# Rotating query and key tiles in three GpSimd instructions, two of them held until VectorE's last two-operand instruction

## The chip, the cores and the metric

The kernel runs on one core of a Trainium2 chip. The metric is the device time of one execution in microseconds (us). TensorE (PE) multiplies matrices, VectorE (DVE) and GpSimd (POOL) do elementwise work and reductions, ScalarE (ACT) applies functions and copies, SyncE (SP) issues DMAs.

## The reference

Attention with rotary positions over 4 batches of 8 heads, 576 tokens and 64 values a head, followed by a gated feed-forward layer.

```
q_rot, k_rot = rotate(q), rotate(k)      # x1*cos - x2*sin, x1*sin + x2*cos
scores = scale * q_rot @ k_rot^T
attn = exp(scores - max(scores)); attn = attn / (sum(attn) + 1e-9)
x = attn @ v                             # heads side by side: 512 wide
h = relu(x @ w_in)
conv = 3-tap convolution of h along the tokens, weights conv_w
out = (h * sigmoid(conv)) @ w_out
```

The feed-forward weights arrive as 64-bit floats and are turned into 32-bit ones on the chip.

## The kernel before

Two heads make a pair; there are 16 pairs (p = 0 to 15). A pair takes five turns: four for 128 query rows of both heads, one for the last 64 rows of both. Turn 5p + s is step s of pair p. In a turn TensorE computes the scores (`emit_S`, tile `sp`), VectorE takes their maxima (`negm`, L264), ScalarE the exponentials (`st` or `str`, L268), TensorE transposes them (`emit_T`, L316), ScalarE copies them out (`pt`, L196), and TensorE multiplies them by v (`emit_E`, L393).

The order is written by hand. `at(turn, rank, fn)` puts work into a table, and the loop at the end of `emit` runs a turn's entries by rising rank; each engine gets its instructions in that order and takes them in that order. Ranks used here: 0 transposes of the exponentials, 0.2 maxima, 0.3 exponentials, 0.4 conversion of weights, 0.45 transposes of rotated q and k, 0.5 scores of the next turn, 1.7 normalisation (L411), 4.5 reciprocal row sums (L362 to L364), 16 loads, 18 rotations.

Up to turn 25 (`WIDE` is 26) the turns also carry the conversion of the weights: for each piece of 512 columns a ScalarE step (L599) and four VectorE steps (L602, L608, L613, L618). Pieces of the last weight matrix are then split: ScalarE makes `wouth` (L685) and GpSimd the remainder `woutl` in four instructions (L682). The split is deferred by a few steps of the table after the piece's L618.

The rotation of pair p (`rope`, tiles `rq` and `rk`) is done by GpSimd in place. The two half-vectors of a head are multiplied by a table of cosines and sines (L187, six pieces of 192 columns), then one product is added to the other (L190, three pieces of 192 columns). VectorE transposes the result into `qT` (L229) and `kT` (L232, with two small ones at L236), which the scores of the pair read. With n = 5p, for pairs 2 to 5 the rotations of both tensors stand at turn n-6, rank 18, the transpose of q at turn n-4 and that of k at turn n-2. Each of `rq` and `rk` has one buffer: the load for pair p+1 waits for the transpose of pair p.

Of the kernel before, what the change touches and what calls it, by code (L numbers as in the profile page):

```python
# [12 lines left out]
ALU = mybir.AluOpType  # L13
# [7 lines left out]
def attention_moe_kernel(ctx, tc, q, k, v, w_in, conv_w, w_out, tab, tabx, out):  # L21
    nc = tc.nc
# [8 lines left out]
    XW = HS + 2  # L31
# [29 lines left out]
    tabt = keep.tile([128, S // 32, 2, 32], F32, name="tabt")  # L61
# [14 lines left out]
    late = {"tail": False, "u": 0}  # L76
# [5 lines left out]
    def defer(k, fn, rank=1):  # L82
        due.setdefault(slot[0] + k, []).append((rank, len(due.get(slot[0] + k, [])), fn))
# [9 lines left out]
    def after(fn):  # L93
        if "m" in psum or late["n"] + 1 == WIDE:
            fn()
        else:
            at(late["n"] + 1, 0.35, fn)

    def spare(n):
        a = free["at"]  # L100
        if "m" in psum or late["n"] + 1 == WIDE:
            return t_tile()[:, 0:n]
        assert a + n <= 960
        free["at"] = a + n
        return free["ps"][:, a:a + n]
# [8 lines left out]
    def m_tile():  # L114
        if late["tail"]:
            return psum["t"].tile([128, 512], F32, tag="mt", name="mt")
        ps = m_pair()
        pair["k"] ^= 1
        return ps[1 - pair["k"]]

    raw = {}
# [21 lines left out]
    def load(p, part):  # L143
        b, hp = divmod(p, NPB)
        x = raw[p, part] = p1.tile([128, S // 32, 2, 32], F32, tag="r" + part, name="r" + part)
        for h in range(2):
            y = (q if part == "q" else k)[b, 2 * hp + h].rearrange("(c i) d -> i c d", i=32)
            for g in range(2):
                r = slice(64 * h + 32 * g, 64 * h + 32 * g + 32)
                nc.sync.dma_start(out=x[r].rearrange("i c e d -> i c (e d)"), in_=y)  # L150
# [3 lines left out]
    def load_v(p):  # L154
        b, hp = divmod(p, NPB)
        t = vmain[p] = p1.tile([128, 2, 4, D], F32, tag="vm", name="vm", bufs=2)
        for h in range(2):
            nc.sync.dma_start(out=t[:, h], in_=v[b, 2 * hp + h, 0:512, :].rearrange("(t p) d -> p t d", p=128))
            nc.sync.dma_start(out=vrem[p % 2][64 * h:64 * h + 64, h, :], in_=v[b, 2 * hp + h, 512:S, :])
# [23 lines left out]
    def rope(p, part):  # L183
        x = raw[p, part]
        for a in range(0, 18, 3):
            y = x[:, a:a + 3]
            nc.gpsimd.tensor_tensor(out=y, in0=y, in1=tabt[:, a:a + 3], op=ALU.mult)  # L187
        for a in range(0, 18, 6):
            y = x[:, a:a + 6]
            nc.gpsimd.tensor_tensor(out=y[:, :, 0, :], in0=y[:, :, 0, :], in1=y[:, :, 1, :], op=ALU.add)  # L190

    QT, KT = {}, {}

    def evac(eng, out, in_, sc=None):
# [30 lines left out]
    def emit_TQ(p, part):  # L225
        qk_tiles(p)
        x = raw.pop((p, part))[:, :, 0, :]
        if part == "q":
            nc.vector.transpose(out=QT[p].rearrange("p (c i) -> p c i", i=32), in_=x)  # L229
        else:  # L230
            kt = KT[p].rearrange("p (c i) -> p c i", i=32)
            nc.vector.transpose(out=kt[:, 2:20], in_=x)  # L232
            if p * STEPS < WIDE:
                for h in range(2):
                    r = slice(64 * h, 64 * h + 64)
                    nc.vector.transpose(out=krem[p % 2][r, r].rearrange("p (c i) -> p c i", i=32), in_=x[r, 16:18])  # L236
            if p * STEPS + STEPS > WIDE:
                nc.vector.transpose(out=kt[:, 0:2], in_=x[:, 16:18])
# [3 lines left out]
    negm, sums = {}, {}  # L242
# [113 lines left out]
    rb = {}  # L356
    rds = {}

    def emit_rinv(p):
        rv = rvc[p % 2]  # L360
        rt = p1.tile([128, 32], F32, tag="rt", name="rt")
        nc.vector.scalar_tensor_tensor(out=rv[:, 0:9], in0=sums[p], scalar=1e-9, in1=sums[p], op0=ALU.add, op1=ALU.max)  # L362
        nc.vector.reciprocal(out=rv[:, 0:9], in_=rv[:, 0:9])
        nc.vector.transpose(out=rt, in_=rv)  # L364
        d = scr.tile([9, 128], F32, tag="d", name="rd")
        for i in range(0, 128, 32):
            nc.sync.dma_start(out=d[:, i:i + 32], in_=rt[i:i + 9, :])
        rds[p] = d
# [15 lines left out]
    def x_at(sl, e):  # L384
        return xT[:, sl, e, :] if sl < NSLOT - NK else xmore[sl][e]

    def emit_E(p, j, a=0, n=XW):
        b, hp = divmod(p, NPB)
        xp = m_tile()[:, 0:n] if "m" in psum else spare(n)
        o = (S - XW) * j  # L390
        for i in range(5):
            for h in range(2):
                nc.tensor.matmul(  # L393
                    out=xp[64 * h:64 * h + 64, :],
                    lhsT=vmain[p][:, h, i, :] if i < 4 else vrem[p % 2][:, h, :],
                    rhs=pt[:, 2 * i + h if i < 4 else 8, o + a:o + a + n],
                    start=(i == 0),
                    stop=(i == 4),
                )
        if a == 0:  # L400
            xns[p, j] = p2.tile([128, XW], F32, tag="xn", name="xn", bufs=4)
        xn = xns[p, j]
        after(lambda: nc.scalar.activation(out=xn[:, a:a + n], in_=xp, func=AF.Copy))

        def norm():
            if plain(2 * b):
                dst = xraw[hp, j] = xtra.tile([128, XW], F32, tag="x", name="xr")
            else:
                xslot[b, hp, j] = free_slots.pop(0)
                dst = xn  # L410
            nc.vector.tensor_tensor(out=dst, in0=xn, in1=rb[p][:, o:o + XW], op=ALU.mult)  # L411

        def high():
            nc.scalar.activation(out=x_at(xslot[b, hp, j], 0), in_=xn, func=AF.Copy)  # L414

        def low():
            sl = xslot[b, hp, j]
            nc.gpsimd.tensor_tensor(out=x_at(sl, 1), in0=xn, in1=x_at(sl, 0).bitcast(F32), op=ALU.subtract)  # L418

        def both():  # L420
            norm()
            if not plain(2 * b):
                defer(1, lambda: (high(), low()))

        norms[p, j] = both

    def plain(blk):
        return blk < 2
# [163 lines left out]
    def to_f32(pool, bufs, w64, n, t=None):  # L592
        w32 = w64.bitcast(I32).rearrange("p (n t) -> p n t", t=2)
        h, l = w32[:, :, 1], w32[:, :, 0]
        if t is None:
            t = pool.tile([128, n], I32, tag="wt", name="wt", bufs=bufs)[0:w64.shape[0]]

        def first():
            nc.scalar.activation(out=t.bitcast(F32), in_=h.bitcast(F32), func=AF.Abs)  # L599

        def clamp():
            nc.vector.tensor_scalar(  # L602
                out=t.bitcast(F32), in0=t.bitcast(F32), scalar1=bits(F32_TINY), scalar2=bits(F32_HUGE),
                op0=ALU.max, op1=ALU.min,
            )

        def shift():
            nc.vector.tensor_scalar(  # L608
                out=t, in0=t, scalar1=3, scalar2=0x3FFFFFFF, op0=ALU.logical_shift_left, op1=ALU.bitwise_and
            )  # L610

        def low():
            nc.vector.scalar_tensor_tensor(  # L613
                out=t, in0=l, scalar=29, in1=t, op0=ALU.logical_shift_right, op1=ALU.bitwise_or
            )

        def third(w):
            nc.vector.scalar_tensor_tensor(  # L618
                out=w.bitcast(I32), in0=h, scalar=-(1 << 30), in1=t, op0=ALU.bitwise_and, op1=ALU.bitwise_or
            )  # L620

        return first, clamp, shift, low, third

    def bits(i):
        import struct

        return struct.unpack("<f", struct.pack("<I", i))[0]
# [98 lines left out]
    WIDE = 26  # L726
# [16 lines left out]
    def at(n, rank, fn):  # L743
        plan.setdefault(n, []).append((rank, len(plan.get(n, [])), fn))

    def emit():
        with tc.manual_schedule(engines=engines):
# [30 lines left out]
            for p in range(1, NP):  # L778
                n = STEPS * p
                early = n - 10 >= WIDE - 1  # L780
                for i, part in enumerate("qk"):
                    if p > 1:
                        at(max(n - 10, WIDE) if early else n - 9 + 2 * i, 19.6 if early else 16, lambda p=p, part=part: load(p, part))
                    at(n - 8 + i if early else max(n - 6, 0), 18, lambda p=p, part=part: rope(p, part))
                    at(n - 5 + i * (n - 15 < WIDE) if early else max(n - 4 + 2 * i, 2), 0.45, lambda p=p, part=part: emit_TQ(p, part))
                at(n - 1, 15, lambda p=p: load_v(p))
            for p in range(NP):
                n = STEPS * p
# [45 lines left out]
            n = -1  # L834
# [38 lines left out]
            for u in seq + second + m2_units(t, B * S // 128):  # L873
                u()
                tick()

    emit()


# [43 lines left out]
```

## Time and profile before

| | us |
|---|---|
| median of 3 runs (473.62 to 475.83) | 473.81 |
| profiled execution | 472.73 |
| its span | 470.9 |

| engine | busy us | share of the span |
|---|---|---|
| PE, matmul | 456.7 | 97% |
| DVE | 354.6 | 75% |
| ACT | 327.4 | 70% |
| POOL | 291.7 | 62% |

The profile is of one execution. Its span runs from the first to the last instruction; the execution's time is 1.83 us longer. TensorE was granted its full clock throughout. The work of the changed rotations lies in the first fifth of the span. Releasers, written `<-`, name what ended an engine's idle time.

### The profile page before, as it was taken

Reading aid. Unit: us, or ns where it says so; the run is one execution under the profiler, and the core shown is the slowest. Engines: PE = TensorE matmul, PEld = TensorE weight load, DVE = VectorE, ACT = ScalarE, POOL = GpSimd, SP = SyncE. Lnnn points to the kernel's source line nnn. Section 1 sums busy time; section 2 is a strip of 40 time slices with the busy share of each in tenths; the row PEclk is TensorE's granted clock in tenths of the full one; section 3 lists DMA queues with packets and bytes.
Section 4 is the critical chain, followed back from the end, with each engine's and each line's share of the span. In section 5 each row is a group of like instructions: output and inputs, shape, how many; then the busy total and the mean of one; then the engine's idle time right before and its main releaser. Section 6 shows DMA issues by size and latency. Waiting matters only on the chain.

```text
span 470.9 us, 12238 instructions
## 1 busy us (share of the span) xinstructions
PE 456.7 (97%) x4555; PEld 357.4 (76%) x4555; DVE 354.6 (75%) x648; ACT 327.4 (70%) x940; POOL 291.7 (62%) x471
## 2 busy tenths in 40 slices
PE   8799999989999999999999999999999999999997
PEld 7356656657666878778787979788787878899886
DVE  6999999968999897678686777866765748368921
ACT  3889879978897878868696868768686844244400
POOL 0977696996889695997949393929420333133510
PEclk9999999999999999999999999999999999999999
DMA  9989667453370715126161716133010000100011
GB/s 242 242 187 227 159 149 147 121 140 82 98 194 6 139 38 124 32 58 102 39 139 39 139 38 139 39 97 79 27 49 27 25 26 3 46 23 24 0 68 45
DMA packets 103631, 42.33 MB, mean 90 GB/s; under 512 B 94524, under 2 KB 97876, under 8 KB 103572
## 3 DMA queue, kind: packets, MB, share of 16 engines
q1 hardware_dynamic: 103120, 41.20, 37.4%
q8 instruction: 36, 0.59, 0.5%
q10 hardware_dynamic: 452, 0.35, 0.2%
q14 instruction: 23, 0.19, 0.1%
HBM read 36.74 MB, written 4.79 MB: 88 GB/s over the span
## 4 chain that ended last, share of the span: by engine, by line
PE 70%; ACT 11%; DVE 10%; POOL 3%; DMA 3%; issue 1%; SPq 1%; ACTq 0%; DVEq 0%; POOLq 0%
PE sp L256 11%; PE mt L552 11%; PE pm L572 10%; PE pm L393 10%; PE pm L460 9%; PE mt L460 7%; PE tp L316 6%; ACT st L268 4%; PE pm L450 4%; DVE negm L264 3%; ACT pt L196 3%; PE sp L393 2%; POOL rk L187 2%; DVE c L481 1%; DMA rk<-k 1%
## 5 line engine op out<-in xcount | busy, mean ns | idle before, releaser
L264 DVE TENSOR_REDUCE negm<-sp 128x1 f32<-128x576 f32 x144 | 102.5, 747 | 23.7 <-PE sp L256 18.9
L268 ACT ACTIVATE st<-sp,negm 128x576 f32<-128x576 f32 x128 | 93.8, 742 | 27.9 <-DVE negm L264 24.0
L256 PE MATMUL sp<-kT,qT 64*128 64x288 f32 (+4 forms) x556 | 94.8, 450 | 0.5 <-ACT pt L196 0.3
L196 ACT ACTIVATE pt<-tp 128x512 f32<-128x512 f32 (+3 forms) x176 | 84.5, 534 | 5.6 <-PE tp L316 5.0
L481 DVE SCALAR_TENSOR_TENSOR c<-rr,cw,c 128x288 f32<-128x288 f32 x128 | 79.7, 623 | 4.2
L187 POOL TENSOR_TENSOR rq<-rq,tabt 128x192 f32<-128x192 f32 x90 | 61.1, 711 | 27.8 <-DMA rq<-q 25.8
L499 POOL TENSOR_TENSOR gm<-c,gm 128x288 fp32r<-128x288 f32 (+4 forms) x72 | 45.7, 640 | 49.8 <-ACT gm L498 49.5
L256 PEld LDWEIGHTS sp<-kT,qT 64*128 64x128 f32 (+1 forms) x556 | 44.8, 174 | 22.6 <-issue 8.6
L187 POOL TENSOR_TENSOR rk<-rk,tabt 128x192 f32<-128x192 f32 x90 | 58.9, 688 | 2.5 <-DVE negm L264 1.8
L316 PEld LDWEIGHTS tp<-idf,st 64*128 64x128 f32 x1024 | 41.4, 139 | 21.4 <-ACT st L268 10.1
L316 PE MATMUL tp<-idf,st 64*128 64x64 f32 x1024 | 47.7, 227 | 5.7 <-ACT st L268 4.9
L393 PE MATMUL pm<-pt,vm 128*64 128x290 f32 x368 | 49.8, 411 | 0.4 <-ACT pt L196 0.4
L572 PE MATMUL pm<-wouth,gm 64*128 64x256 f32 x512 | 49.6, 284 | 0.0
L490 DVE SCALAR_TENSOR_TENSOR c<-c,rr 128x288 f32<-128x288 f32 x64 | 37.2, 602 | 10.3 <-ACT c L487 10.3
L479 DVE TENSOR_SCALAR c<-rr,cw 128x288 f32<-128x288 f32 x56 | 24.4, 436 | 22.7 <-ACT rr L471 22.4
L572 PEld LDWEIGHTS pm<-wouth,gm 64*128 64x128 f32 x512 | 41.4, 186 | 0.0
L418 POOL TENSOR_TENSOR xT<-xn,xT 128x290 fp32r<-128x290 f32 x18 | 16.4, 911 | 37.4 <-ACT xT L414 37.4
L393 PEld LDWEIGHTS pm<-pt,vm 128*64 128x64 f32 x368 | 25.5, 136 | 17.8 <-ACT pt L196 1.0
L460 PE MATMUL pm<-xT,wh 128*128 128x290 f32 x176 | 37.0, 302 | 0.0
L572 PE MATMUL pm<-woutl,gm 64*128 64x256 f32 x256 | 36.8, 278 | 0.0
L487 ACT ACTIVATE c<-c 128x288 f32<-128x288 f32 x64 | 28.5, 445 | 11.4 <-DVE c L481 11.4
L450 PE MATMUL pm<-xr,wr 128*128 128x290 f32 x128 | 34.5, 417 | 0.0
(137 smaller groups left out, 971.3 us busy)
## 6 DMA issues: line engine op xcount, KB each, us to landing
rq<-q SPq DMA_DIRECT2D x60, 144.0 KB
rk<-k SPq DMA_DIRECT2D x60, 144.0 KB
w<-moe_w_in SPq DMA_DIRECT2D x8, 512.0 KB
vm<-v SPq DMA_DIRECT2D x32, 128.0 KB
rb<-rd SPq DMA_DIRECT2D x16, 144.0 KB
out<-oh SPq DMA_DIRECT2D x18, 128.0 KB
rb<-rd SPq DMA_DIRECT2D x16, 128.0 KB
w<-moe_w_out SPq DMA_DIRECT2D x4, 512.0 KB
```

Of the source, the lines that this page charges most:

```text
L187: nc.gpsimd.tensor_tensor(out=y, in0=y, in1=tabt[:, a:a + 3], op=ALU.mult)
L196: nc.scalar.activation(out=out, in_=in_, func=AF.Copy, scale=1.0 if sc is None else sc)
L256: nc.tensor.matmul(out=out, lhsT=qt[64 * h:64 * h + 64, c], rhs=kt[64 * h:64 * h + 64, a:a + n], start=True, stop=True)
L264: reds.setdefault((p, s), []).append(lambda: nc.vector.tensor_reduce(out=nm, in_=sc, axis=AX.XY if len(sc.shape) == 3 else AX.X, op=ALU.ma ...
L268: lambda: nc.scalar.activation(out=dst, in_=sc, func=AF.Exp, bias=nm, scale=1.0, accum_out=sm)
L316: nc.tensor.transpose(ps[r][:, 64 * k:64 * k + 64], x[i], idf[i, i])
L393: nc.tensor.matmul(out=xp[64 * h:64 * h + 64, :], lhsT=vmain[p][:, h, i, :] if i < 4 else vrem[p % 2][:, h, :], rhs=pt[:, 2 * i + h if i < ...
L450: nc.tensor.matmul(out=ps[:, 0:XW], lhsT=raws[kk, half][:, gs], rhs=xraw[kk, j], start=(kk == 0), stop=(kk == NK - 1))
L460: nc.tensor.matmul(out=ps[:, 0:XW], lhsT=w, rhs=x_at(xs, e), start=(i == 0), stop=(i == n - 1))
L481: nc.vector.scalar_tensor_tensor(out=c, in0=r[:, j + e:j + e + HS], scalar=cw[:, 8 * e + f:8 * e + f + 1], in1=c, op0=ALU.mult, op1=ALU.add,)
L552: nc.tensor.matmul(out=ops[tt][:, 0:width], lhsT=g_tile(tt, f, e), rhs=w[:, f, cols], start=(f == 0 and i == 0), stop=(f == NF - 1 and i = ...
L572: nc.tensor.matmul(out=ps[r][:, 0:256], lhsT=g_tile(tt, f, e)[rows], rhs=w[rows, f, cols], start=(f == 0 and i == 0), stop=(f == NF - 1 an ...
```

## The change

For pairs 2 to 5 the nine instructions of a tensor become three: two products of 576 columns (called a and b below) and one sum of 576 columns (c). The three stand at turns of their own, just ahead of the turn's maxima: for q at n-7, n-5 and n-4, for k at n-4, n-3 and n-2. Before, all stood at the end of turn n-6. b and c get an explicit dependency on the last VectorE instruction recorded so far among those wrapped in `port` (L362, L411 and the four weight conversion steps); a has none. Pair 1 and pairs 6 to 15 keep the nine instructions.

```diff
+    def port(ins):
+        late["v"] = ins
+        return ins
+
+    def gated(ins):
+        tc.add_manual_dep(
+            ins.ins, late["v"].ins.name, mybir.DependencyInfo(mybir.DependencyClass.Sync, mybir.DependencyReason.DATA), reason="port"
+        )
+
+    def rope_by_three(p, part):
+        def mult(i):
+            y = raw[p, part][:, 9 * i:9 * i + 9]
+            return nc.gpsimd.tensor_tensor(out=y, in0=y, in1=tabt[:, 9 * i:9 * i + 9], op=ALU.mult)
+
+        def add():
+            y = raw[p, part]
+            return nc.gpsimd.tensor_tensor(out=y[:, :, 0, :], in0=y[:, :, 0, :], in1=y[:, :, 1, :], op=ALU.add)
+
+        return lambda: mult(0), lambda: mult(1), add
...
-            nc.vector.tensor_tensor(out=dst, in0=xn, in1=rb[p][:, o:o + XW], op=ALU.mult)
+            port(nc.vector.tensor_tensor(out=dst, in0=xn, in1=rb[p][:, o:o + XW], op=ALU.mult))
...
-                    at(n - 8 + i if early else max(n - 6, 0), 18, lambda p=p, part=part: rope(p, part))
+                    if 1 < p and n <= WIDE:
+                        a, b, c = rope_by_three(p, part)
+                        if part == "q":
+                            at(n - 7, 0.191, a)
+                            at(n - 5, 0.19, lambda b=b: gated(b()))
+                            at(n - 4, 0.19, lambda c=c: gated(c()))
+                        else:
+                            at(n - 4, 0.191, a)
+                            at(n - 3, 0.19, lambda b=b: gated(b()))
+                            at(n - 2, 0.19, lambda c=c: gated(c()))
+                    else:
+                        at(n - 8 + i if early else max(n - 6, 0), 18, lambda p=p, part=part: rope(p, part))
```

GpSimd's instructions before, from the q tensor of pair 4 to the first rotations of pair 5; what stands in brackets are the semaphores waited for (`DMAHW` for a load, `Activation` for ScalarE, `DVE` and `Pool` for the engines):

```order
L187 TENSOR_TENSOR rq<-rq,tabt 128x192 [waits DMAHW3_49,DMAHW2_49,DMAHW4_49,DMAHW1_49,DVE_49]
L187 TENSOR_TENSOR rq<-rq,tabt 128x192 x5
L190 TENSOR_TENSOR rq<-rq 128x6x32 [waits Pool_49] x3
L187 TENSOR_TENSOR rk<-rk,tabt 128x192 [waits DMAHW3_49,DMAHW2_49,DMAHW4_49,DMAHW1_49,DVE_49]
L187 TENSOR_TENSOR rk<-rk,tabt 128x192 x5
L190 TENSOR_TENSOR rk<-rk 128x6x32 [waits Pool_49] x3
L682 TENSOR_TENSOR woutl<-wf,wouth 128x128 [waits Activation_49]
L682 TENSOR_TENSOR woutl<-wf,wouth 128x128 x3
L187 TENSOR_TENSOR rq<-rq,tabt 128x192 [waits DMAHW6_49,DMAHW7_49,DMAHW1_49,DMAHW0_49]
```

The same place now, to the end of the k tensor of pair 5 (L704 was L682, L204 is the product and L208 the sum):

```order
L204 TENSOR_TENSOR rk<-rk,tabt 128x576 [waits DMAHW3_49,DMAHW2_49,DMAHW4_49,DMAHW1_49]
L204 TENSOR_TENSOR rk<-rk,tabt 128x576 [waits DVE_49]
L704 TENSOR_TENSOR woutl<-wf,wouth 128x128 [waits Activation_49]
L704 TENSOR_TENSOR woutl<-wf,wouth 128x128 x3
L208 TENSOR_TENSOR rk<-rk 128x18x32 [waits Pool_49]
L204 TENSOR_TENSOR rq<-rq,tabt 128x576 [waits DMAHW6_49,DMAHW7_49,DMAHW1_49,DMAHW0_49]
L704 TENSOR_TENSOR woutl<-wf,wouth 128x128 [waits Activation_49]
L704 TENSOR_TENSOR woutl<-wf,wouth 128x128 x3
L204 TENSOR_TENSOR rq<-rq,tabt 128x576
L208 TENSOR_TENSOR rq<-rq 128x18x32 [waits DVE_49,Pool_49]
L204 TENSOR_TENSOR rk<-rk,tabt 128x576 [waits DMAHW6_49,DMAHW7_49,DMAHW5_49,DMAHW0_49]
L204 TENSOR_TENSOR rk<-rk,tabt 128x576 [waits DVE_49]
```

Three groups of `woutl`, which wait for ScalarE, stood behind whole rotations before. Now the first stands between b and c of pair 4's k, the second between a and b of pair 5's q, and the third, one row below the end of this piece, between b and c of pair 5's k.

VectorE's order is the same in both. These are its rows of turn 18 in the changed kernel (L624 and L630 were L602 and L608, L252 and L256 were L232 and L236, L284 was L264):

```order
L284 TENSOR_REDUCE negm<-sp 128x1
L624 TENSOR_SCALAR wt<-wt 128x512 [waits Activation_49]
L630 TENSOR_SCALAR wt<-wt 128x512 [waits DVE_49]
L252 STREAM_TRANSPOSE kT<-rk 128x576 [waits DMAHW3_49,DMAHW2_49,DMAHW4_49,DMAHW1_49,Pool_49]
L256 STREAM_TRANSPOSE kr_96<-rk 64x64 x2
L284 TENSOR_REDUCE negm<-sp 128x1 [waits PE_49]
```

The transpose of k waits for GpSimd in this turn, and the next turn's maximum stands behind it.

## Rows read from the trace of the kernel before

**Rows 1.** Two stretches: length; busy PE, PEld, DVE, ACT, POOL; clock; DMA share; GB/s.
```profile
20.00:98.00 78.00, 72.01 (x832) 46.18 (x833) 74.21 (x125) 67.64 (x182) 64.46 (x98) 1.00 0.72 164
106.00:370.00 264.00, 262.92 (x2904) 208.82 (x2904) 204.05 (x360) 207.58 (x608) 180.80 (x291) 1.00 0.35 77
```
**Rows 2.** ScalarE's waits, 20 to 72 us: total us, times, longest.
```profile
ACT st L268 <- DVE negm L264: 5.4, 8, 1.1
```
**Rows 3.** VectorE's groups, 20 to 98 us: busy us, mean ns | idle before.
```profile
L613 DVE SCALAR_TENSOR_TENSOR wt<-w,wt 128x512 int32<-128x512 int32 x10 | 8.5, 850 | 0.2
L608 DVE TENSOR_SCALAR wt<-wt 128x512 int32<-128x512 int32 x10 | 6.3, 633 | 0.2
L602 DVE TENSOR_SCALAR wt<-wt 128x512 f32<-128x512 f32 x10 | 6.3, 627 | 0.0
L411 DVE TENSOR_TENSOR xr<-xn,rb 128x290 f32<-128x290 f32 x8 | 6.1, 765 | 0.0
L618 DVE SCALAR_TENSOR_TENSOR wr<-w,wt 128x512 int32<-128x512 int32 x7 | 6.0, 856 | 0.1
L362 DVE SCALAR_TENSOR_TENSOR rvc<-sums 128x9 f32<-128x9 f32 x5 | 2.8, 557 | 0.0
```
**Rows 4.** Single lines: count, ns min/median/max, first and last start us, forms.
```profile
L613 DVE SCALAR_TENSOR_TENSOR wt<-w,wt x12: 674/884/1106, 11.1 to 91.7; 128x512 int32<-128x512 int32 x12
L411 DVE TENSOR_TENSOR xn<-xn,rb x24: 451/454/846, 115.3 to 389.4; 128x290 f32<-128x290 f32 x24
L362 DVE SCALAR_TENSOR_TENSOR rvc<-sums x16: 122/555/760, 30.4 to 381.4; 128x9 f32<-128x9 f32 x16
L187 POOL TENSOR_TENSOR rq<-rq,tabt x90: 580/656/1102, 11.8 to 322.1; 128x192 f32<-128x192 f32 x90
L418 POOL TENSOR_TENSOR xT<-xn,xT x18: 792/812/1252, 127.8 to 390.8; 128x290 fp32r<-128x290 f32 x18
```
**Rows 5.** GpSimd in order of time: start us, us, what [idle before <-releaser].
```profile
58.24 4.17 POOL L187 TENSOR_TENSOR rq<-rq,tabt 128x192 f32<-128x192 f32 x6 [4.34 <-DMA rq<-q]
...
74.23 1.93 POOL L682 TENSOR_TENSOR woutl<-wf,wouth 128x128 fp32r<-128x128 f32 x4 [3.97 <-ACT wouth L685]
```
**Rows 6.** VectorE in order of time, turns 18 to 24.
```profile
72.38 1.41 DVE L264 TENSOR_REDUCE negm<-sp 128x1 f32<-128x576 f32 x2
73.72 0.41 DVE L602 TENSOR_SCALAR wt<-wt 128x512 f32<-128x512 f32 x1
74.16 0.43 DVE L608 TENSOR_SCALAR wt<-wt 128x512 int32<-128x512 int32 x1
74.51 0.77 DVE L232 STREAM_TRANSPOSE kT<-rk 128x576 f32<-128x576 f32 x1
...
76.08 0.76 DVE L264 TENSOR_REDUCE negm<-sp 128x1 f32<-128x576 f32 x1 [0.43 <-PE sp L393]
...
86.59 1.41 DVE L264 TENSOR_REDUCE negm<-sp 128x1 f32<-128x576 f32 x2
...
92.46 0.77 DVE L232 STREAM_TRANSPOSE kT<-rk 128x576 f32<-128x576 f32 x1
...
93.81 0.72 DVE L264 TENSOR_REDUCE negm<-sp 128x1 f32<-128x576 f32 x1
```
**Rows 7.** ScalarE in order of time, turns 17 to 24.
```profile
73.50 0.65 ACT L685 ACTIVATE wouth<-wf 128x512 fp32r<-128x512 f32 x1
...
78.09 0.75 ACT L268 ACTIVATE str<-sp,negm 128x576 f32<-128x576 f32 x1
...
80.70 0.63 ACT L685 ACTIVATE wouth<-wf 128x512 fp32r<-128x512 f32 x1
...
88.03 0.74 ACT L268 ACTIVATE st<-sp,negm 128x576 f32<-128x576 f32 x1
...
89.81 0.64 ACT L685 ACTIVATE wouth<-wf 128x512 fp32r<-128x512 f32 x1
...
94.77 0.74 ACT L268 ACTIVATE str<-sp,negm 128x576 f32<-128x576 f32 x1
```

More of the change, by code (lines that the diff above doesn't have):

```diff
@@ L361, in emit_rinv @@
         rt = p1.tile([128, 32], F32, tag="rt", name="rt")
-        nc.vector.scalar_tensor_tensor(out=rv[:, 0:9], in0=sums[p], scalar=1e-9, in1=sums[p], op0=ALU.add, op1=ALU.max)
+        port(nc.vector.scalar_tensor_tensor(
+            out=rv[:, 0:9], in0=sums[p], scalar=1e-9, in1=sums[p], op0=ALU.add, op1=ALU.max
+        ))
         nc.vector.reciprocal(out=rv[:, 0:9], in_=rv[:, 0:9])
@@ L601, in clamp @@
         def clamp():
-            nc.vector.tensor_scalar(
+            port(nc.vector.tensor_scalar(
                 out=t.bitcast(F32), in0=t.bitcast(F32), scalar1=bits(F32_TINY), scalar2=bits(F32_HUGE),
                 op0=ALU.max, op1=ALU.min,
-            )
+            ))
         def shift():
-            nc.vector.tensor_scalar(
+            port(nc.vector.tensor_scalar(
                 out=t, in0=t, scalar1=3, scalar2=0x3FFFFFFF, op0=ALU.logical_shift_left, op1=ALU.bitwise_and
-            )
+            ))
         def low():
-            nc.vector.scalar_tensor_tensor(
+            port(nc.vector.scalar_tensor_tensor(
                 out=t, in0=l, scalar=29, in1=t, op0=ALU.logical_shift_right, op1=ALU.bitwise_or
-            )
+            ))
         def third(w):
-            nc.vector.scalar_tensor_tensor(
+            port(nc.vector.scalar_tensor_tensor(
                 out=w.bitcast(I32), in0=h, scalar=-(1 << 30), in1=t, op0=ALU.bitwise_and, op1=ALU.bitwise_or
-            )
+            ))
         return first, clamp, shift, low, third
```

## The prediction

> **What bounds the kernel now.** I read the busy shares by stretch first, because the changed rotations lie in 20 to 98 us and the rest of the program only follows. There VectorE works 74.21 of 78.00 us and TensorE 72.01, while from 106 us on TensorE works 262.92 of 264 [rows 1]. Behind 98 us nothing can be gained or lost: whatever turn 25 is early or late by arrives at the end one to one. In front, TensorE idles 6.0 us in all. Then I asked who is waited for: ScalarE's exponentials waited 5.4 us in eight waits for VectorE's maxima, all before 72 us, that is before turn 18 [rows 2]. From there ScalarE or TensorE is the later one. So VectorE sets the pace at first, and 5.4 us is the most that a quicker VectorE can return.
>
> What slows VectorE is seen in instructions of one size with two durations. L613 takes 674 ns at least and 1106 at most, L362 takes 122 and 760, L411 takes 451 and 846; GpSimd's product of 192 columns takes 580 and 1102 [rows 4]. The differences, 0.4 to 0.6 us, are about the length of one instruction of the other engine. The maxima, which read their input from the score tile, take 1.41 us for two with GpSimd busy [rows 6]. So these VectorE instructions and GpSimd's take turns, each waiting for the other's running instruction, and the maxima don't take part.
>
> **The change part by part.**
>
> *Length of the new instructions.* From 580 ns for 192 columns and 792 for 290 [rows 4] a column costs 2.16 ns, so 576 columns cost 0.792 + 286 × 0.00216 = 1.41 us, an estimate by a straight line. That is as long as two maxima. Three make 4.2 us a tensor against 9 × 0.58 = 5.2.
>
> The Trainium skill (GPSIMD Engine Reference, Performance versus the Vector engine) gives about 2.6 cycles an element at 1.2 GHz for two inputs, hence an estimate of 1.25 us for 576, without a start cost. The trace disagrees at 192 columns, 0.58 against 0.42 by that figure. With 1.25 us the held instructions would end before the maxima do, and the sum below would be about 0.6 us lower.
>
> *What VectorE loses to GpSimd now.* From the means [rows 3] and the undisturbed durations (L613 674 and the like L618 the same, L411 451, L362 122 [rows 4]; L602 410, L608 430 [rows 6]): 10 × 0.176 + 10 × 0.203 + 10 × 0.217 + 8 × 0.314 + 7 × 0.18 + 5 × 0.435 = 11.9 us. About 0.9 belongs to the rotations of pairs 1 and 6, which stay; 11 are in play.
>
> *What it loses then, at the free places.* A held instruction starts some 0.08 us behind its releaser (`woutl` starts at 74.23, `wouth` ends at 74.15 [rows 5, 7]) and ends 1.49 behind it; the maxima end 1.33 behind it, since VectorE's instructions overlap by about 0.08 [rows 6]. About eight of the sixteen stand so and hold the next VectorE instruction up by 0.16: 1.3 us. The others start behind L362, whose two short followers give half a microsecond more, or are dealt with below. The eight a are not held. Those of k follow c directly, and in turn n-4 c starts behind the L362 of the turn before, so a still runs for 1.1 us when the maxima are over: three of them (pair 5's is below) cost 3.3. Those of q start when their load lands, as now [rows 5], wherever VectorE then is: 0 to 1.41 each, I take 0.85 for three, 2.5. Together 7.1: VectorE saves 3.9. Only what falls into the eight waits counts, since elsewhere VectorE isn't last; I take half, 1.9. The bounds are 5.4 gained and, with all eight a at 1.41 and sixteen overhangs (13.8, half of the 2.8 more), 1.4 lost.
>
> On this rests how GpSimd and VectorE share. The Trainium skill (SBUF — State Buffer, Who interferes with whom) says that the one which starts first keeps the shared port for its whole instruction and the other stands still. The trace agrees, 1106 against 674 ns beside pieces of 580. If they shared at half speed instead, an a behind the maxima would cost 0.67 and not 1.1, and the sum would be 1.3 lower.
>
> *First group of `woutl`.* c of pair 4's k now stands behind the group of 1.93 us that waits for `wouth`, ended at 74.15 [rows 5, 7]. c then runs from 76.16 to 77.57. VectorE's transpose of k in turn 18 started at 74.51 [rows 6] and must wait for c: 3.1 us of a stopped VectorE, with the maximum of turn 19 behind it. That maximum was 0.43 late by TensorE, so it moves by 2.67, from 76.08 to 78.75, and ends at 79.5. Its exponential started at 78.09 [rows 7] with 1.25 us in hand. It comes 1.4 late. ScalarE works without a break from there to the next exponentials, so nothing is given back: +1.4 (0 if ScalarE reaches `wouth` 2 us sooner, 3.1 without the slack).
>
> *Second group.* It waits for the `wouth` that ends at 81.33 [rows 7], so b of pair 5's q runs from about 83.3, not beside the maxima of turn 21 but behind them. b, c and then k's a each meet one of VectorE's L608, L613 and L411, at most 1.41 each, 4.2; I take 3.0, since each has begun when VectorE comes. By rows 3 these three lose 0.7 now. +2.3 (0 to 3.5). The maxima of turn 22 end at 88.00 and the exponential starts at 88.03 [rows 6, 7], so there is no slack.
>
> *Third group.* `wouth` ends at 90.45 [rows 7], `woutl` at 92.46, c at 93.87; the transpose of turn 23 started at 92.46 [rows 6], so it moves by 1.45. The maximum of turn 24 ends at 94.53 and its exponential starts at 94.77, so 0.24 are absorbed: +1.2 (0 to 1.5).
>
> *Sum.* 1.4 + 2.3 + 1.2 − 1.9 = +3.0 us. Loads move with the transposes that free their buffers, a microsecond or three, and the rotations of pair 6 have two turns in hand. Against the profiled execution, 472.73, that is 475.7. The median is 1.08 above it, so I predict 473.81 + 3.0 = 476.8.
>
> **The rivals.**
> 1. *The held instructions pay and the three stalls are absorbed.* For it: 5.4 us of waits that end with VectorE, all before the first group. Against it: the exponential of turn 22 has 0.03 us in hand. If the three places cost 1 us together and the gain is 3.5, the time is 471.3.
> 2. *A wash.* VectorE's gain arrives in full at 3.5 and the stalls cost about as much: 473.8. For it: TensorE and ScalarE have gaps of their own to absorb in.
> 3. *The hold loses its place.* GpSimd runs behind, so that b and c start when GpSimd is free, not at the maxima. Then 24 long instructions meet VectorE wherever it is. At 0.85 each this is 20 us against 11, half of it on the path: +4.7, with the stalls of 4.9 some 483, and a partial case 480. It decides once GpSimd is later than one turn. Against it: GpSimd then works 8.4 us for the two tensors of a pair, and five turns take some 17.
> 4. *The dependencies change nothing,* because the data come later than the hold anyway. The order shows it for two of the sixteen, c of pair 4's k and b of pair 5's q, which wait for `woutl` and no longer for VectorE. It would not differ from 2.
>
> **How the numbers follow.** Forecast 0.48, rival 1 0.24, rivals 2 and 4 0.20, rival 3 0.08. A difference under 0.5% (2.4 us) can't be told from no change. Slower by more: rival 3 and most of the forecast, 0.53; within: 0.23; faster: 0.24. The range goes from 471.0, rival 1 with a little more, to 480.5, the forecast with the stalls near their upper ends. The forecast's own range is 475 to 480.
>
> **What would show it.** Right: a group GpSimd 576 columns wide at 1.4 us undisturbed; VectorE's transpose of k in turns 18 and 23 idle before, released by GpSimd's sum, some 3 and 1.5 us; L613 or L618 of turn n-4 near 1.7 to 2.1 us; the means of L602, L608 and L362 lower. ScalarE's waits for the maxima fall before turn 17 and rise behind it. Wrong: a transpose in turn 18 that starts within half a microsecond of its turn's weight steps, or a maximum of turn 24 earlier than at 93.8.

## The result, and the profile after

The changed kernel takes 477.99 us (median of 12 runs, 476.10 to 480.76), the kernel before 474.17 in the 12 runs beside them: ratio 1.0091, interval 1.0070 to 1.0112, or 3.8 us slower by the medians. 476.8 was predicted. The profiled execution took 479.51.

The two stretches of [rows 1], in the profile after:

```profile
20.00:98.00 78.00, 70.70 (x803) 44.90 (x801) 68.65 (x116) 65.42 (x173) 44.97 (x47) 0.98 0.74 164
106.00:370.00 264.00, 262.67 (x2894) 207.00 (x2896) 204.05 (x357) 206.19 (x599) 185.82 (x299) 1.00 0.36 79
```

The second stretch is as it was. In the first, GpSimd works 45.0 us instead of 64.5, VectorE 68.7 instead of 74.2, and TensorE does less work too (803 matmuls, not 832): fewer busy engines, and a later end. This execution was late before any changed instruction: turn 4's maximum starts at 27.58 us, before at 25.01 (in a second profile of the changed kernel, experiment 11, at 25.03). So kernels are compared below by the time from the start of that maximum to the start of turn 25's maxima. In the kernel before it is 95.81 − 25.01 = 70.80:

```profile
25.01 0.76 DVE L264 TENSOR_REDUCE negm<-sp 128x1 f32<-128x576 f32 x1
...
95.81 1.41 DVE L264 TENSOR_REDUCE negm<-sp 128x1 f32<-128x576 f32 x2
```

VectorE of the changed kernel in order of time (columns as in [rows 6]; L284 was L264, L635 L613, L640 L618, L249 and L252 L229 and L232):

```profile
27.58 0.76 DVE L284 TENSOR_REDUCE negm<-sp 128x1 f32<-128x576 f32 x1
...
29.10 1.90 DVE L640 SCALAR_TENSOR_TENSOR wr<-w,wt 128x512 int32<-128x512 int32 x1
...
35.02 1.75 DVE L635 SCALAR_TENSOR_TENSOR wt<-w,wt 128x512 int32<-128x512 int32 x1
...
79.24 0.78 DVE L252 STREAM_TRANSPOSE kT<-rk 128x576 f32<-128x576 f32 x1 [2.54 <-POOL rk L208]
...
80.42 0.76 DVE L284 TENSOR_REDUCE negm<-sp 128x1 f32<-128x576 f32 x1
...
86.61 1.42 DVE L284 TENSOR_REDUCE negm<-sp 128x1 f32<-128x576 f32 x2 [1.37 <-PE sp L415]
...
99.24 0.78 DVE L252 STREAM_TRANSPOSE kT<-rk 128x576 f32<-128x576 f32 x1 [2.54 <-POOL rk L208]
...
102.64 1.41 DVE L284 TENSOR_REDUCE negm<-sp 128x1 f32<-128x576 f32 x2
```

From 27.58 to 102.64 it is 75.06, 4.26 more. Up to turn 18 the changed kernel is 0.74 ahead; the two transposes of k that stand idle for 2.54 us (turns 18 and 23) turn that round. What they wait for, GpSimd in order of time:

```profile
31.08 1.40 POOL L204 TENSOR_TENSOR rq<-rq,tabt 128x576 f32<-128x576 f32 x1 [0.63 <-DVE wr L640]
...
34.81 1.41 POOL L204 TENSOR_TENSOR rk<-rk,tabt 128x576 f32<-128x576 f32 x1
...
75.96 1.89 POOL L704 TENSOR_TENSOR woutl<-wf,wouth 128x128 fp32r<-128x128 f32 x4 [2.94 <-ACT wouth L707]
77.80 1.41 POOL L208 TENSOR_TENSOR rk<-rk 128x576 f32<-128x576 f32 x1
...
95.66 2.19 POOL L704 TENSOR_TENSOR woutl<-wf,wouth 128x128 fp32r<-128x128 f32 x4 [2.38 <-ACT wouth L707]
97.81 1.40 POOL L208 TENSOR_TENSOR rk<-rk 128x576 f32<-128x576 f32 x1
```

Each time GpSimd stood idle for over 2 us with `woutl`, which waits for ScalarE, at the head of its queue, and the sum c behind it. The delay reaches ScalarE: before, its exponentials' waits for maxima all ended by 72 us [rows 2], and now there are three behind:

```profile
81.21 0.74 ACT L288 ACTIVATE str<-sp,negm 128x576 f32<-128x576 f32 x1 [1.29 <-DVE negm L284]
...
93.16 0.74 ACT L288 ACTIVATE st<-sp,negm 128x576 f32<-128x576 f32 x1 [1.38 <-DVE negm L284]
...
101.34 0.74 ACT L288 ACTIVATE str<-sp,negm 128x576 f32<-128x576 f32 x1 [1.58 <-DVE negm L284]
```

VectorE's groups, 20 to 104 us, which answer to [rows 3] (L624 was L602, L630 L608, L433 L411, L382 L362):

```profile
L635 DVE SCALAR_TENSOR_TENSOR wt<-w,wt 128x512 int32<-128x512 int32 x10 | 9.3, 929 | 0.2
L640 DVE SCALAR_TENSOR_TENSOR wr<-w,wt 128x512 int32<-128x512 int32 x7 | 8.4, 1202 | 0.1
L624 DVE TENSOR_SCALAR wt<-wt 128x512 f32<-128x512 f32 x10 | 6.1, 608 | 0.0
L630 DVE TENSOR_SCALAR wt<-wt 128x512 int32<-128x512 int32 x10 | 5.0, 496 | 0.2
L433 DVE TENSOR_TENSOR xr<-xn,rb 128x290 f32<-128x290 f32 x8 | 4.6, 578 | 0.0
L382 DVE SCALAR_TENSOR_TENSOR rvc<-sums 128x9 f32<-128x9 f32 x4 | 0.6, 161 | 0.0
```

L630, L433 and L382, beside which GpSimd is now held, fell by 0.14, 0.19 and 0.40 us each. L635 and L640 rose by 0.08 and 0.35: there the unheld a of q and of k run. The undisturbed durations of the prediction make these groups' loss 10.1 us; it was 11.9.

One thing was not forecast: TensorE's clock. In turn 18 TensorE stood idle for 1.36 us, and soon after its granted clock was 0.50 of full (1.2 instead of 2.4 GHz) for some 3.4 us. First a window of 3 us there (the column ahead of the last two is the clock), then TensorE in order of time:

```profile
81.00:84.00 3.00, 3.00 (x19) 1.64 (x17) 2.94 (x6) 2.47 (x8) 0.00 (x0) 0.50 0.99 190
```

```profile
80.16 1.39 PE L276 MATMUL sp<-kT,qT 64*128 64x512 f32 x4 [1.36 <-DVE kT L252]
...
83.01 1.73 PE L276 MATMUL sp<-kT,qT 64*128 64x512 f32 x4
```

The same four matmuls took 1.12 us in the first experiment's kernel, where the clock did not fall.

### The profile page after: what moved, and what is told of

Its sections match the earlier page's. It is cut to its first block, busy times and chain, and to the rows that moved or that the text cites. A ratio compares the mean times of both kernels' runs of the same rounds, so it can differ in the third digit from the quotient of the medians.

```text
span 477.6 us, 12197 instructions
## 1 busy us (share of the span) xinstructions
PE 457.7 (96%) x4555; PEld 357.4 (75%) x4555; DVE 354.1 (74%) x648; ACT 327.8 (69%) x940; POOL 276.3 (58%) x423
## 4 chain that ended last, share of the span: by engine, by line
PE 68%; DVE 9%; ACT 8%; POOL 5%; DMA 4%; issue 3%; SPq 1%; ACTq 0%; DVEq 0%; POOLq 0%
PE sp L276 11%; PE mt L574 11%; PE pm L594 10%; PE pm L415 10%; PE pm L482 9%; PE mt L482 7%; PE tp L336 5%; PE pm L472 4%; ACT st L288 3%; DVE negm L284 2%; ACT pt L216 2%; DMA rk<-k 2%; POOL rk L187 2%; DVE c L503 1%; PE sp L415 1%
## 5 line engine op out<-in xcount | busy, mean ns | idle before, releaser
L284 DVE TENSOR_REDUCE negm<-sp 128x1 f32<-128x576 f32 x144 | 102.5, 748 | 23.7 <-PE sp L276 18.5
L288 ACT ACTIVATE st<-sp,negm 128x576 f32<-128x576 f32 x128 | 94.0, 743 | 26.2 <-DVE negm L284 22.3
L187 POOL TENSOR_TENSOR rq<-rq,tabt 128x192 f32<-128x192 f32 x66 | 44.0, 700 | 20.4 <-DMA rq<-q 20.4
L512 DVE SCALAR_TENSOR_TENSOR c<-c,rr 128x288 f32<-128x288 f32 x64 | 38.3, 620 | 10.1 <-ACT c L509 10.1
L187 POOL TENSOR_TENSOR rk<-rk,tabt 128x192 f32<-128x192 f32 x66 | 42.9, 683 | 3.4 <-DMA rk<-k 2.6
```

Source lines behind the costliest of these rows:

```text
L284: reds.setdefault((p, s), []).append(lambda: nc.vector.tensor_reduce(out=nm, in_=sc, axis=AX.XY if len(sc.shape) == 3 else AX.X, op=ALU.ma ...
L288: lambda: nc.scalar.activation(out=dst, in_=sc, func=AF.Exp, bias=nm, scale=1.0, accum_out=sm)
```

## The experiments

Theory: holding b and c pays, and the groups of `woutl` left between the three parts of a rotation take back more than that. First rival: long instructions cost VectorE more than short ones, held or not. Each edit is against the kernel that is named. "Loss" is the time by which VectorE's instructions that GpSimd slows (the six of [rows 3]) exceed their undisturbed durations, from turn 4 to turn 25, summed from the trace.

| kernel | us, median | ratio to before (95%) | turn 4 to 18 | to 25 | loss |
|---|---|---|---|---|---|
| before | 474.17 | | 47.37 | 70.80 | 11.3 |
| changed | 477.99 | 1.0091 (1.0070 to 1.0112) | 46.63 | 75.06 | 9.6 |
| changed, again | 479.54 | 1.0100 (1.0074 to 1.0127) | 45.82 | 74.62 | 8.2 |
| 1 `woutl` behind | 473.48 | 0.9995 (0.9980 to 1.0010) | 46.75 | 69.98 | 8.2 |
| 2 three, old place | 484.84 | 1.0229 (1.0204 to 1.0255) | 57.12 | 80.67 | 18.5 |
| 3 as 1, no hold | 486.30 | 1.0255 (1.0211 to 1.0298) | 54.92 | 80.33 | 17.6 |
| 4 as 1, k's a held | 472.58 | 0.9966 (0.9951 to 0.9981) | 45.52 | 68.99 | 7.6 |
| 5 pairs 2 and 3 only | 473.94 | 0.9990 (0.9973 to 1.0007) | 47.09 | 70.33 | 10.6 |
| 6 as 1, nine pieces | 472.30 | 0.9940 (0.9920 to 0.9961) | 46.16 | 69.25 | 9.2 |
| 7 as 1, group 2 between | 475.59 | 1.0022 (1.0003 to 1.0040) | 46.34 | 70.56 | 10.6 |
| 8 as 1, group 1 between | 475.93 | 1.0024 (1.0006 to 1.0042) | 46.58 | 72.05 | 8.7 |
| 9 as 1, group 3 between | 475.99 | 1.0018 (1.0001 to 1.0035) | 46.49 | 71.58 | 9.9 |
| 10 as 6, k's a held | 470.46 | 0.9914 (0.9892 to 0.9936) | 44.75 | 67.78 | 7.3 |

The kernel before had medians of 474.2 to 474.9 in the runs beside each. The ratios are worked out from those runs one by one, and can differ by 0.1% from the quotient of the medians. Stretches and losses are of one profiled execution each: two of the changed kernel differ by 0.44 us at turn 25 and by 1.4 us in the loss.

**1. The groups of `woutl` one turn later,** behind that turn's a, b or c; the rest is the changed kernel.

```diff
-                defer(2, lambda: (high(), low()))
+                def split():
+                    high()
+                    if late["n"] + 1 < WIDE:
+                        at(late["n"] + 1, 0.195, low)
+                    else:
+                        low()
+
+                defer(2, split)
```

> The changed kernel, but each group of woutl is recorded one turn later, behind the long GpSimd instructions of that turn; everything else stands. Theory A (the loss is VectorE's transposes of q and k standing still behind woutl and the sum c): in the changed kernel's trace the three places cost 2.0, 0.5 and 2.5 us at the following exponentials, 5.0 in all. Without them this runs at 478.0 - 5.0 = 473.0 us, 0.2% under the kernel before (ratio 0.993 to 1.002), the transposes of turns 18 and 23 start within 0.2 us of VectorE's earlier work, and ScalarE's waits for the maxima after 76 us (4.3 us in the changed kernel) are under 1. Theory B (long GpSimd instructions cost VectorE more than short ones, and woutl is only where it shows): 477 to 478, ratio 1.007.

The loss of 3.8 us is gone. VectorE in turns 18 to 23:

```profile
74.75 0.77 DVE L252 STREAM_TRANSPOSE kT<-rk 128x576 f32<-128x576 f32 x1
...
82.31 1.42 DVE L284 TENSOR_REDUCE negm<-sp 128x1 f32<-128x576 f32 x2 [0.97 <-PE sp L415]
...
86.28 1.42 DVE L284 TENSOR_REDUCE negm<-sp 128x1 f32<-128x576 f32 x2 [0.31 <-PE sp L415]
...
89.75 1.42 DVE L284 TENSOR_REDUCE negm<-sp 128x1 f32<-128x576 f32 x2 [1.11 <-PE sp L415]
```

The transpose of k in turn 18 doesn't wait, and the next turns' maxima wait for TensorE. So the place of `woutl` is what made the change slower. What is left of the gain is 0.8 us in the stretch and can't be told from nothing in the time.

**2. Three instructions at the old place, none held** (an edit of the kernel before).

```diff
-        for a in range(0, 18, 3):
-            y = x[:, a:a + 3]
+        u, w = (9, 18) if 1 < p and STEPS * p <= WIDE else (3, 6)
+        for a in range(0, 18, u):
+            y = x[:, a:a + u]
...
-        for a in range(0, 18, 6):
-            y = x[:, a:a + 6]
+        for a in range(0, 18, w):
+            y = x[:, a:a + w]
```

> The kernel before, with the rotations of pairs 2 to 5 in three instructions of 576 columns at their old place and held by nothing. Theory A: no transpose stands still, since woutl stays behind whole rotations, but each VectorE instruction that meets a long one waits up to 1.4 us. In the changed kernel an unheld a cost 1.2, 1.1, 1.2, 0.8, 1.1 us where it was met. Per pair some five of VectorE's instructions meet one at about 1.0, 5 us against 2.8 now; four pairs, half on the path: +4.5, 478.6 us (476 to 481), ratio 1.009. Theory B (number and length of GpSimd's instructions is all, and 8 us less of GpSimd work is a gain): 472, ratio 0.995 or less.

10.6 us slower, over twice what was expected. First GpSimd, then VectorE, in order of time (a line number is one higher here than in the kernel before):

```profile
36.87 3.23 POOL L188 TENSOR_TENSOR rk<-rk,tabt 128x576 f32<-128x576 f32 x2 [1.99 <-DMA vr<-v]
40.18 1.75 POOL L191 TENSOR_TENSOR rk<-rk 128x576 f32<-128x576 f32 x1
```

```profile
36.96 1.87 DVE L614 SCALAR_TENSOR_TENSOR wt<-w,wt 128x512 int32<-128x512 int32 x1
38.86 1.79 DVE L619 SCALAR_TENSOR_TENSOR wr<-w,wt 128x512 int32<-128x512 int32 x1
```

The engines take turns: each VectorE step of about 0.7 us stands still while one of 1.41 us ends. VectorE's loss grows from 11.3 to 18.5 us, and these 7.2 are most of the 9.9 in the stretch; taking half of it for the path was wrong. With VectorE this late its loss arrives nearly whole: from turn 4 to turn 25 ScalarE waits 13.2 us for the maxima, where it was 5.4. A part of the rest may be TensorE's, whose granted clock was 0.50 in two windows of this execution, the first of which began ahead of turn 4's maximum at 27.88:

```profile
24.00:29.00 5.00, 4.97 (x43) 3.08 (x45) 4.02 (x8) 3.52 (x11) 2.27 (x4) 0.50 1.27 171
61.00:64.00 3.00, 2.94 (x19) 1.25 (x16) 2.97 (x6) 2.41 (x8) 0.00 (x0) 0.50 0.87 266
```

**3. The first experiment's kernel without the hold.** Order and lengths stay, the added dependencies go.

```diff
     def gated(ins):
-        tc.add_manual_dep(
-            ins.ins, late["v"].ins.name, mybir.DependencyInfo(mybir.DependencyClass.Sync, mybir.DependencyReason.DATA), reason="port"
-        )
+        pass
```

> The first run's kernel without the explicit dependencies: the same GpSimd order and the same three instructions, which now run as soon as their data are there. Theory A (the hold is what keeps the long instructions beside the maxima): as the kernel with three unheld ones at the old place, 80 us from turn 4 to turn 25, 484 us, ratio 1.02. Theory B (the new places in the order do it, the hold adds little): 474 to 476.

12.8 us slower than with the hold, and like experiment 2. To issue the instructions at turns of their own does nothing by itself; the hold is worth all that the length costs. Here, too, the clock was low in the mean (0.985 to 0.992); how much of the price that is, is not shown.

**4. The first of k held as well,** in turn n-4 behind the weight steps, ahead of the next maxima (on experiment 1).

```diff
-                            at(n - 4, 0.191, a)
+                            at(n - 4, 0.44, lambda a=a: gated(a()))
```

> As the first of these four, and the first product of k is also held, behind the last weight step of its turn, so that it runs beside VectorE's transpose of q. Theory A: the instruction it met lost 1.1 us in three or four pairs; now L411 behind the transpose loses about 0.6. VectorE gains 2 us in all, half of it on the path: 472.2 us, 1 us under the first of the four, ratio 0.996. Rival (ScalarE and TensorE set the pace once the stalls are gone): the same as the first, within 0.4 us.

1.0 us less in the stretch than experiment 1, the time 0.34% under the kernel before. For pair 4 the hold ends too soon: the last wrapped instruction recorded by then is L630, which ends at 68.21, and a transpose and L433 still follow ahead of the maxima. First GpSimd (the trace puts the release down to a load), then VectorE:

```profile
68.28 1.42 POOL L204 TENSOR_TENSOR rk<-rk,tabt 128x576 f32<-128x576 f32 x1 [1.49 <-DMA w<-moe_w_out]
```

```profile
67.78 0.43 DVE L630 TENSOR_SCALAR wt<-wt 128x512 int32<-128x512 int32 x1
68.12 0.77 DVE L249 STREAM_TRANSPOSE qT<-rq 128x576 f32<-128x576 f32 x1
68.81 1.21 DVE L433 TENSOR_TENSOR xr<-xn,rb 128x290 f32<-128x290 f32 x1
```

The product starts beside the transpose and L433 pays 0.76 us. A dependency holds an instruction until a place in the program, and whoever comes behind that place meets it.

**5. Only pairs 2 and 3 by three** (on the changed kernel), so that no group of `woutl` can stand between.

```diff
-                    if 1 < p and n <= WIDE:
+                    if 1 < p < 4:
```

> The changed kernel with three held instructions for pairs 2 and 3 alone; pairs 4 and 5 have nine again at the old place, so no group of woutl stands inside a rotation. Theory A: only the early gain is left, which the trace of the changed kernel shows as 0.8 us less from turn 4 to turn 18 (about half of it from these two pairs): 473.7, ratio 0.999 (0.995 to 1.003). Theory B: half of the changed kernel's loss stays, 476.1, ratio 1.004.

No difference in the time, 0.5 us less in the stretch. With fewer pairs there is no gain that could be told from nothing, and nothing is lost: both agree with the theory.

**6. Nine held pieces** (on experiment 1): each third is issued as three instructions of 192 columns, of which the first carries the dependency.

```diff
-            y = raw[p, part][:, 9 * i:9 * i + 9]
-            return nc.gpsimd.tensor_tensor(out=y, in0=y, in1=tabt[:, 9 * i:9 * i + 9], op=ALU.mult)
+            ys = [slice(9 * i + 3 * k, 9 * i + 3 * k + 3) for k in range(3)]
+            return [
+                nc.gpsimd.tensor_tensor(out=raw[p, part][:, y], in0=raw[p, part][:, y], in1=tabt[:, y], op=ALU.mult)
+                for y in ys
+            ][0]
...
```

The sum c is cut in the same way.

> The kernel of the first run (each woutl group a turn later), with each of the three instructions cut into three of 192 columns again; only the first of each third is held, so place and hold stay and only the length goes. Measure besides the time: the start of turn 25's maxima less that of turn 4's, 70.0 us in the first run, 70.8 before the change. Theory A (the hold pays, not the length): a held third takes 1.76 us and not 1.41 and overhangs the maxima by 0.5, 0.35 more in some eight places, 2.8 us; an unheld one stops VectorE for at most 0.58 and not 1.1, 0.5 less in six places, 3.0 us. The same as the first run within 0.7 us, 473.5, ratio 0.9995 (0.998 to 1.002). Theory B (fewer, longer instructions are what pays): 474.5 to 476.

0.60% under the kernel before, where three long ones gave nothing; neither theory had that. First ScalarE's waits for the maxima, 20 to 98 us (5.4 in [rows 2], 3.9 in experiment 1; L293 and L289 were L288 and L284), then the products of q:

```profile
ACT st L293 <- DVE negm L289: 0.7, 2, 0.4
```

```profile
L205 POOL TENSOR_TENSOR rq<-rq,tabt x24: 582/592/1042, 29.6 to 81.4; 128x192 f32<-128x192 f32 x24
```

GpSimd works 52.7 us from turn 4 to 25, against 43.3 in the changed kernel: its own time bought nothing. VectorE's loss in all is not what fell either, 9.2 us against 8.2 in experiment 1. It is spread otherwise: there six VectorE steps lose 0.84 to 1.23 us each, 6.3 together, here none loses more than 0.44. That small delays are absorbed behind VectorE and large ones are not would fit ScalarE's waits; it is argued from one execution of each. So length costs time though the pieces are held, as the first rival has it, some 0.5%; why is open.

**7 to 9. One group of `woutl` left between,** the others behind (on experiment 1): the second (`i != 9`), the first (8) and the third (10).

```diff
-                    if late["n"] + 1 < WIDE:
+                    if late["n"] + 1 < WIDE and i != 9:
```

> The first run's kernel, with the second group of woutl left where the changed kernel has it, between a and b of pair 5's q. Theory A (the prediction's term was right for this place alone: b falls behind the maxima of turn 21, and b, c and k's a each stop one VectorE instruction): +2.3 us against the first run, 72.3 us from turn 4 to turn 25, 475.8 us, ratio 1.004. In the changed kernel the place cost only 0.5, since VectorE was late already (its maxima waited 1.4 us for TensorE) and b ran beside them. Theory B (the place is harmless as such): +0.5 or less, 70.5, 474.0.

> The first run's kernel, with the first group of woutl left between b and c of pair 4's k. Theory A: VectorE's transpose of k in turn 18 stands still for 2.5 us as in the changed kernel, and turn 20 comes 2.0 us later: 72.0 from turn 4 to turn 25, 475.5 us, ratio 1.0035. Theory B (ScalarE's slack of 1.25 us takes more of it, and the changed kernel's 2.0 has other causes): 1.0 us or less, 474.5.

> The first run's kernel (each woutl group a turn later), with the third group alone left between b and c of pair 5's k. From turn 4 to turn 25 the first run took 69.98 us, the first group alone added 2.07, the second 0.58, all three together in the changed kernel 5.08. Theory A (the places add up): the third alone adds 2.4, 72.4 us, and the time is 476, ratio 1.004. Theory B (the prediction's term): 1.2, 71.2 us, 474.7, ratio 1.002; the rest in the changed kernel would come from the three together.

At turn 25, against experiment 1: group 2 +0.58, group 1 +2.07, group 3 +1.60, together 4.25. All three at once cost 75.06 − 69.98 = 5.08, and by the second profile 4.64. The difference is about what two profiles of one kernel differ by. The times tell less of a difference between the groups: by the ratios to the kernel before, group 1 costs 1.4 us over experiment 1, group 2 1.3 and group 3 1.1, each with an interval of about 1.1 to either side. With one group in place the transpose of k waits once; the waits of VectorE, 70 to 104 us, of experiments 8 and 9:

```profile
DVE kT L252 <- POOL rk L208: 2.5, 1, 2.5
```

```profile
DVE kT L252 <- POOL rk L208: 1.7, 1, 1.7
```

Group 2 is the surprise. VectorE of experiment 7 in turns 21 to 23, and the exponential behind:

```profile
84.48 1.08 DVE L630 TENSOR_SCALAR wt<-wt 128x512 int32<-128x512 int32 x1
85.59 1.79 DVE L635 SCALAR_TENSOR_TENSOR wt<-w,wt 128x512 int32<-128x512 int32 x1
...
88.00 0.97 DVE L433 TENSOR_TENSOR xr<-xn,rb 128x290 f32<-128x290 f32 x1
88.89 1.41 DVE L284 TENSOR_REDUCE negm<-sp 128x1 f32<-128x576 f32 x2
...
91.26 1.41 DVE L284 TENSOR_REDUCE negm<-sp 128x1 f32<-128x576 f32 x2
```

```profile
90.34 0.74 ACT L288 ACTIVATE st<-sp,negm 128x576 f32<-128x576 f32 x1 [1.51 <-DVE negm L284]
```

b, c and a do meet one step each, VectorE loses 2.4 us more than in experiment 1, and ScalarE waits 1.51. But turn 23's maxima follow turn 22's after 2.37 us, where in experiment 1 it was 3.47 with a wait of 1.11 for TensorE: TensorE had run ahead meanwhile, and most of the loss came back a turn later. How much is left is less sure than +0.58: up to turn 21 the two kernels are the same, and there this execution is 0.44 ahead, so from turn 21 to 25 the group costs 1.0 (14.38 against 13.36). The stretch is theory B's, the time lies between the two (ratio 1.0022, where A had 1.004); 0.6 to 1.3 us is what the record supports.

**10. Nine held pieces and k's first held** (experiments 6 and 4 together).

> Nine held pieces, woutl a turn later, and k's first third also held, behind the last weight step of its turn, beside VectorE's transpose of q. Theory A (the parts add up): holding k's first product took 1.0 us off the kernel with long instructions, where it stopped VectorE for 1.1; a short piece stops it for 0.58 at most, so about 0.4 here: 68.8 us from turn 4 to turn 25 against 69.25, 472 us, ratio 0.993. Rival (nothing is left to gain, VectorE no longer sets the pace): 69.25 within 0.3. Slower than 69.6 would mean that the place beside the transpose is worse than the one behind c.

470.46 us against 474.70 beside it, 0.86% under the kernel before and 7.5 us under the changed one. In the stretch that is 1.5 us less than experiment 6, where 0.4 was expected; by the ratios it is 1.2, with 1.4 to either side, and experiment 6's profile had TensorE's clock at 0.50 for the first 3 us of its stretch, so the size of this step is open. The fault of experiment 4 is milder with short pieces: the product of pair 4's k starts at the same place, and L433 (L438 here) is undisturbed, while the six pieces take 0.75 us each instead of 0.58. First GpSimd, then VectorE:

```profile
66.53 4.50 POOL L205 TENSOR_TENSOR rk<-rk,tabt 128x192 f32<-128x192 f32 x6 [0.84 <-DVE wt L635]
```

```profile
66.36 0.77 DVE L254 STREAM_TRANSPOSE qT<-rq 128x576 f32<-128x576 f32 x1
67.06 0.42 DVE L438 TENSOR_TENSOR xr<-xn,rb 128x290 f32<-128x290 f32 x1
```

**11. The changed kernel again,** nothing altered, for TensorE's clock.

> The changed kernel once more, with nothing altered, for more pairs of time and granted clock. In its first profile TensorE stood idle from 78.80 to 80.16 us, behind the transpose of k in turn 18, and from 80.9 to 84.3 us it was granted 0.50 of its full clock. Theory A, this fall of the clock is part of the loss: the executions with a mean granted clock of 0.998 and more lie 1 us or more under those of 0.996 and less, and a profile in which the clock does not fall behind turn 18 gives under 74.5 us from the maximum of turn 4 to that of turn 25, where the first gave 75.06. Theory B, the other engines hide it: the two kinds of executions differ by under 0.5 us, and such a profile gives 74.9 to 75.2 us again. By A the stalls of VectorE alone cost some 1 us less than the 3.8 us measured.

It doesn't decide. The six timed executions had a mean clock of 0.993 to 0.996, and none was at full clock, so the test by a profile without the fall could not be made. In this profile the clock fell again behind turn 18 (a window, then TensorE in order of time):

```profile
77.00:80.00 3.00, 3.00 (x15) 1.17 (x15) 2.38 (x4) 1.73 (x5) 0.07 (x1) 0.50 0.45 101
```

```profile
76.66 2.04 PE L276 MATMUL sp<-kT,qT 64*128 64x512 f32 x4 [1.42 <-DVE kT L252]
```

Of both batches, three executions at 0.998 and more took 476.10, 476.51 and 478.47 us, and fifteen at 0.988 to 0.996 had the median 479.39. That alone does not speak for theory A, for the two kinds differ in the kernel before as well, which has no such stall: of its 82 timed executions beside the experiments the 50 at 0.998 and more had the median 474.15 us, the 32 at 0.996 and less 475.38. The mean clock doesn't tell where the clock fell. Shown is who brings it about here: the clock fell to 0.50 behind turn 18 in all three profiles in which that turn's transpose waits (changed twice, experiment 8), and in none of experiments 1, 7 and 9, where it doesn't.

## Why the prediction was right or wrong

*Slower, by about 3 us: right,* with the mechanism named: 476.8 forecast, 477.99 measured. Experiment 1 shows that the loss comes from the three places of `woutl`. The terms were less good than the sum, and that they add up so closely is in part luck.

*Length.* Right: sixteen products of 576 columns have medians of 1407 and 1408 ns, 1.41 was estimated. The Trainium skill's 2.6 cycles an element (GPSIMD Engine Reference, Performance versus the Vector engine) give an estimate of 2.17 ns a column, and the trace agrees: from 192 columns (580 ns) to 576 (1407) a column costs 2.15. The 1.25 us is too low here too by the start cost that it left out, some 0.17.

*VectorE's saving of 3.9 us, half of it on the path: too large, and mostly in the second factor.* By the same groups and undisturbed durations the changed kernel saves 1.8 (11.9 to 10.1). By the table its two profiles save 1.7 and 3.1, and experiment 1, without the stalls, 3.1 (11.3 to 8.2). Of that only 0.8 had arrived at turn 25, a quarter: VectorE stood idle for 5.4 us of the stretch in place of 3.3, so another engine became the later one more often. Up to turn 18 three profiles give 0.6 to 1.6. What is not saved is with the unheld ones: L640, at 1202 ns beside them, loses 3.7 us alone, 1.2 of it to the a of pair 2's q (the 1.90 at 29.10). The a of k behaves as priced. It runs from 34.81 to 36.22, and L635 takes 1.75 instead of 0.67, a loss of 1.08 (1.1 forecast). So the trace agrees with the lock on the port that the Trainium skill describes (SBUF — State Buffer, Who interferes with whom), and not with sharing at half speed, by which 0.67 would have been lost.

*First group, +1.4.* Right in each step: the transpose waited 2.54 us (3.1 forecast), the exponential 1.29 (1.4). Alone it cost 2.07. What was not in the sum is the half clock behind it, and how much of the 0.7 more is its doing is not shown.

*Second group, +2.3: the weakest term.* Alone it cost 0.6 to 1.3. "There is no slack" was true of turn 22: VectorE lost 2.4 us and ScalarE waited 1.51. It was not true of turn 23, where the maxima had 1.11 us to wait for TensorE, and about that much came back. The prediction looked for slack at the next consumer and ended there. In the changed kernel itself the first stall had already moved turn 21, whose maxima waited 1.37 us for TensorE, until 86.61, so that b, from 86.59, met no weight step.

*Third group, +1.2.* Right in kind, low in size: 1.60 alone, 1.58 of wait at the exponential in the changed kernel. VectorE reaches the transpose earlier behind `wouth` than in the kernel before, so more of c is still to come.

*The sum.* By the stretches of the single edits −0.82 + 2.07 + 0.58 + 1.60 = +3.4, against +3.0 by −1.9 + 1.4 + 2.3 + 1.2, and +4.3 and +3.8 in the two profiles. The gain was taken too large by 1.1 and the second group too dear by 1.7 (1.0 by the times), the other two groups too cheap by 0.7 and 0.4: the errors nearly cancelled.

*The rivals.* 1 and 2 fell, since at least two of the three stalls weren't absorbed. 3 did not happen, for the hold kept its place, but experiments 2 and 3 show its mechanism, at +10 us and more instead of +4.7: its loss was about right (20 us forecast, 18.5 in experiment 2), its half on the path was not. 4 is refuted by experiment 3.

## What to carry to other kernels

Two engines that take turns, as VectorE and GpSimd do here, can cost each other nearly a whole instruction: hold the less urgent engine until the other does something that doesn't take part, and keep its pieces short rather than few. Fewer instructions on an engine that isn't last gained nothing here. When work is spread out on an engine that takes its queue in order, look for every instruction in the queue that waits for somebody else; between the parts of a chain it becomes a part of the chain. And follow a delay past its first consumer: it is lost only as far as nobody has a wait to give back in the turns behind.

## What the runs showed of the hardware beyond that

- An explicit dependency costs little: GpSimd's second q instruction starts at 31.08 us, 0.08 behind the end of the L640 that holds it, and with nine pieces ScalarE's waits for maxima fell from 5.4 to 0.7 us.
- TensorE's granted clock can fall to half for 3 to 4 us after an idle of 1.3 to 1.4 us: three of three in turn 18 (1.36, 1.42 and 1.34 us idle). After the idle of turn 23 it did not: 1.52 and 1.53 us in the two profiles of the changed kernel, 1.30 in experiment 9. The length of the idle alone doesn't decide.
- Twenty-four unheld instructions of 1.41 us cost the kernel 10.6 us, though GpSimd then works less than before (45.6 us from turn 4 to 25, against 58.5).
